# A linear-attention and SwiGLU kernel, whose hand-listed order of steps is replaced by another

## The chip, the cores and the metric

The kernel runs on one core of a Trainium2 chip. A core has five engines that work side by side: TensorE (PE, matrix multiply), VectorE (DVE), ScalarE (ACT), GpSimd (POOL) and SyncE (SP), and 16 DMA engines that move data. Each engine works through its own queue in order and waits at an instruction until what it needs is there. The metric is the device time of one execution in microseconds; less is better. Before the change the median of three runs is 202.34 us (202.3 to 202.5).

## The reference

Two stages. The first is a linear attention with a decaying state; the second is a gated feed-forward on its normalised output. There are 4 batches of 8 heads, 768 steps of time and heads of 48 columns, so 3,072 tokens of 384 columns; the feed-forward has 1,536 units.

```python
for t in range(S):                       # per batch and head
    cur = u * kt  (outer)  vt
    y[t] = rt @ (state + cur)
    state = wt[:, None] * state + kt (outer) vt
x  = y as [3072, 384]
xn = x / sqrt(mean(x*x) + 1e-6) * rms_g
out = (silu(xn @ w_gate) * (xn @ w_val)) @ w_out
```

## The kernel before

Time is cut into six superblocks (0 to 5) of 128 steps. A step of work is named `what.n.j`: n is the superblock, j the batch (0 to 3), or, in the feed-forward, one of 12 groups of 128 units. A superblock of 4 batches has 512 tokens, the width of one feed-forward matmul.

For each superblock and batch the attention goes through these steps. `load_r`, `load_k`, `load_v` and `load_w` (L241 to L266) fetch 128 x 384 numbers each, issued by SP; `load_w.0.j` fetches superblocks 0 and 1 at once (384 KB). `ln` (ACT) takes the logarithm of w, `cs_mm` (PE) sums it along time, `exp_r` and `exp_k` (ACT) raise the sums, `r_mul` (DVE) and `k_mul` (DVE, from superblock 1 on POOL) scale r and k by them. `w_tot` (DVE) keeps the decay of the whole block. r and k are turned: in superblocks 0 and 1 by `rk_pe` (PE transposes) and `rk_tr` (an ACT copy out of PSUM), later by a DMA transpose that SP issues, also called `rk_tr`. `q_mm` (PE) multiplies them, `q_mask_e`, `q_copy_o` and `q_mask_o` mask the product (DVE, ACT, and POOL or DVE), `cast_v` makes v bf16, `st_mm` and `st_new` carry the state to the next superblock, and `y_mm` (PE) forms the output. The term with u takes a way of its own: `bonus_mul` (two products on POOL, L452 and L453), `bonus_sum` (DVE), `bonus_v` (POOL); `x_add` (DVE) adds it. `x_sq`, `x_rstd` and `xn_mul` normalise; the result is turned by `xn_pe` and `xn_out` (PE, DVE), in superblocks 4 and 5 by `xn_tr` (DMA transpose on SP) and `xn_gain` (POOL, L586).

The feed-forward of superblock n needs all four turned batches. `gate_mm` and `val_mm` (L598) are three matmuls of 512 columns each, `silu` (ACT) and `h_mul` (DVE, L616) combine them, and `o_mm` (12 matmuls, L630), `o_out` and `out_dma` produce one batch of the output. The weights come in pieces that POOL issues: `load_gv.0.h` for groups 0 to 3 (384 KB as bf16; h is 0 for gate, 1 for val), `load_gv.1.h` for groups 4 to 11 (768 KB), and three `load_wo`. The source is float32 and the DMA casts it.

`warm` (L367) is a matmul of zeros into a PSUM bank that nobody reads.

The order is written out: the string `ORDER` lists all steps, a loop at the end of the kernel calls them one by one, and so every engine's queue has its steps in that order. Waits follow from the data and from the buffers: 8 each of r, k and v tiles, 4 of w, and eight PSUM banks in three rings, "a" and "b" with two banks, "q" with four. `psum` (L218) gives a step the bank of its ring whose last use lies furthest back in the order. ACT holds one function table at a time: logarithm and exponential share one, silu has another, and `act` loads it when needed (L229).

At the head of the old order, SP's queue is r.0.1, w.0.1, k.0.0, k.0.1, w.0.0, r.0.0, v.0.0, w.0.2, w.0.3, k.0.2, v.0.1, r.0.2, r.0.3, v.0.3, v.0.2, r.1.3, k.1.0, k.0.3 and then the rest of superblock 1. POOL's is bonus_mul.0.1, .0.0, .0.2, bonus_v.0.1, .0.0, bonus_mul.0.3, load_gv.0.1, bonus_v.0.2, load_gv.0.0, bonus_v.0.3, load_gv.1.0, k_mul.1.0, k_mul.1.1, load_gv.1.1. The first feed-forward steps of PE are val_mm.0.2, val_mm.0.3, one `warm`, gate_mm.0.2, gate_mm.0.3.

Of the kernel before, what the change touches and what calls it, by code (L numbers as in the profile page):

```python
# [25 lines left out]
load_r.0.1 load_w.0.1 load_k.0.0 load_k.0.1 ln.0.1 warm.31.0 load_w.0.0 ln.0.0 warm.0.0 warm.13.0 warm.28.0  # L26
bonus_mul.0.1 bonus_sum.0.1 load_r.0.0 load_v.0.0 bonus_mul.0.0 load_w.0.2 load_w.0.3 warm.29.0 load_k.0.2 load_v.0.1
load_r.0.2 bonus_mul.0.2 load_r.0.3 load_v.0.3 load_v.0.2 bonus_v.0.1 load_r.1.3 load_k.1.0 cs_mm.0.1 exp_k.0.1
warm.10.0 warm.17.0 warm.33.0 warm.38.0 exp_r.0.1 r_mul.0.1 k_mul.0.1 bonus_sum.0.0 bonus_v.0.0 cs_mm.0.0 exp_r.0.0
ln.0.2 exp_k.0.0 cast_v.0.0 r_mul.0.0 k_mul.0.0 w_tot.0.0 warm.8.0 warm.16.0 warm.12.0 warm.4.0 warm.30.0 w_tot.0.1  # L30
rk_pe.0.1 warm.15.0 warm.14.0 load_k.0.3 bonus_mul.0.3 load_r.1.1 load_r.1.0 load_k.1.1 load_v.1.1 load_r.1.2 ln.0.3
load_k.1.3 warm.20.0 warm.37.0 warm.2.0 warm.22.0 warm.23.0 warm.5.0 warm.3.0 rk_pe.0.0 warm.24.0 load_gv.0.1
load_k.1.2 load_v.1.0 load_w.2.1 warm.25.0 load_v.1.2 load_w.2.0 load_v.1.3 load_r.2.1 load_r.2.0 load_w.2.2 warm.32.0
warm.27.0 st_mm.0.0 st_new.0.0 load_w.2.3 cs_mm.0.2 rk_tr.0.1 q_mm.0.1 warm.19.0 rk_tr.0.0 exp_r.0.2 cast_v.0.1
r_mul.0.2 warm.7.0 cs_mm.0.3 q_mask_e.0.1 q_mm.0.0 warm.6.0 warm.18.0 warm.11.0 warm.26.0 warm.1.0 warm.21.0 warm.36.0
exp_k.0.2 w_tot.0.2 k_mul.0.2 rk_pe.0.2 q_mask_e.0.0 bonus_sum.0.2 bonus_v.0.2 exp_r.0.3 w_tot.0.3 q_mask_o.0.0
r_mul.0.3 warm.39.0 y_mm.0.0 warm.9.0 cs_mm.1.0 cast_v.0.3 q_mask_o.0.1 x_add.0.0 load_k.2.1 load_gv.0.0 cast_v.0.2
# [95 lines left out]
def kernel(  # L133
# [19 lines left out]
    DM = H * D  # L153
# [213 lines left out]
    def warm(n, j):  # L367
        ps = psum("q", ("warm", n, j), [128, DM])
        nc.tensor.matmul(ps.rearrange("p (a x) -> p a x", a=3), lhsT=zero, rhs=bc_mid(zero, 3), start=True, stop=True)
# [279 lines left out]
    for step in ORDER.split():  # L649
        fn, n, j = step.split(".")  # L650
# [32 lines left out]
```

## Time and profile before

| | |
|---|---|
| median of three runs | 202.34 us (202.3, 202.34, 202.5) |
| span of the profiled execution | 202.2 us, first to last instruction |
| PE busy | 192.6 us (95%), 1,600 matmuls |
| DVE, ACT, POOL busy | 146.1, 136.6, 134.3 us |
| read from and written to memory | 25.96 MB and 4.72 MB |
| loads and stores issued by SP | 28.58 MB, 119,504 packets |
| weights issued by POOL | 3.54 MB as written, 2,032 packets |

The profiled execution has no time of its own beside its span of 202.2 us; the runs lie 0.1 to 0.3 us above it.

A row of the timeline gives the start in microseconds from the first instruction, the duration, the engine, the line of the kernel, the operation, what is written and read, the shape, how many of the kind follow each other, and in brackets how long the engine had been idle and what ended that. SPq and POOLq are the queues that issue DMAs. Matmuls overlap in the pipeline, so the distance between the starts of two rows tells what a step costs TensorE, and not the duration of one. In the list of DMA issues the last number is the time from issue to landing. The chain of work that ended last is given as start, length and what it was.

### The profile page before, as it was taken

How to read it: one execution, taken by the hardware profiler on the slowest of the kernel's cores; microseconds unless marked ns; L12 is line 12 of the kernel's file. 1: busy time of each engine (PE TensorE's matmuls, PEld its weight loads, DVE VectorE, ACT ScalarE, POOL GpSimd, SP SyncE). 2: the span in 40 equal slices, each digit the busy share in tenths (PEclk: the TensorE clock that was granted, in tenths of full speed). 3: DMA queues.
4: the chain of work that ended last, by engine and by line, in shares of the span. 5: the costliest groups of instructions: out<-in, count | busy, mean ns of one | idle time of the engine just before them, and what ended most of it. 6: DMA issues, size and time to landing. Idle time of an engine off the chain costs nothing.

```text
span 202.2 us, 4444 instructions
## 1 busy us (share of the span) xinstructions
PE 192.6 (95%) x1600; PEld 113.5 (56%) x1600; DVE 146.1 (72%) x289; ACT 136.6 (68%) x278; POOL 134.3 (66%) x198
## 2 busy tenths in 40 slices
PE   1999988899999999999999999999999999999994
PEld 1564655455666555665556665555555555555562
DVE  6257796658999699987988889788878972146521
ACT  2577699688998557997566978679867764046300
POOL 6527599658789966899789898859898742400000
PEclk9999999999999999999999999999999999999999
DMA  6999999989999999958999978996184022103022
GB/s 152 243 244 177 209 182 202 202 161 201 199 192 221 196 179 238 225 133 194 177 231 245 206 171 195 216 241 134 24 192 112 15 68 71 45 3 117 0 97 99
DMA packets 121566, 32.41 MB, mean 160 GB/s; under 512 B 116420, under 2 KB 120392, under 8 KB 121544
## 3 DMA queue, kind: packets, MB, share of 16 engines
q1 hardware_dynamic: 119504, 28.58, 67.2%
q0 software_dynamic: 2032, 3.54, 9.7%
q8 instruction: 12, 0.20, 0.4%
q14 instruction: 10, 0.08, 0.1%
q10 hardware_dynamic: 8, 0.00, 0.0%
HBM read 25.96 MB, written 4.72 MB: 152 GB/s over the span
## 4 chain that ended last, share of the span: by engine, by line
PE 79%; SPq 8%; DMA 8%; POOL 2%; issue 1%; ACT 0%; POOLq 0%
PE ps_av L598 12%; PE ps_bu L598 12%; PE ps_bv L598 10%; PE ps_au L598 10%; PE ps_qx L630 8%; PE ps_qv L630 7%; SPq L244 7%; DMA wg_sb<-in_moe_w_gate_dram 6%; PE ps_qz L630 5%; PE ps_qu L630 3%; SPq L257 2%; DMA kt<-in_k_dram 2%; PE ps_qu L487 1%; PE ps_av L406 1%; PE ps_qu L515 1%
## 5 line engine op out<-in xcount | busy, mean ns | idle before, releaser
L630 PEld LDWEIGHTS <-ht 128*128 128x128 bf16 x300 | 28.3, 98 | 16.9
L231 ACT ACTIVATE sg<-ps_av 128x512 bf16<-128x512 f32 x38 | 22.7, 598 | 18.4 <-PE ps_av L598 16.8
L616 DVE TENSOR_TENSOR ht<-ps_bu,sg 128x512 bf16<-128x512 f32 x38 | 26.1, 686 | 11.7 <-PE ps_bu L598 8.4
L598 PEld LDWEIGHTS <-wg_sb 128*128 128x128 bf16 x216 | 22.8, 114 | 20.2 <-DMA wg_sb<-in_moe_w_gate_dram 2.1
L598 PEld LDWEIGHTS <-wv_sb 128*128 128x128 bf16 x216 | 23.2, 114 | 19.3 <-DVE xnt L580 0.2
L616 DVE TENSOR_TENSOR ht<-ps_bv,sg 128x512 bf16<-128x512 f32 x34 | 23.3, 686 | 12.2 <-PE ps_bv L598 8.8
L452 POOL TENSOR_TENSOR ruk<-rt,kt 128x384 f32<-128x384 f32 x24 | 24.0, 1000 | 11.1 <-DMA kt<-in_k_dram 6.0
L598 PE MATMUL ps_av<-xnt,wg_sb 128*128 128x512 bf16 x114 | 30.9, 380 | 0.4 <-DMA wg_sb<-in_moe_w_gate_dram 0.4
L231 ACT ACTIVATE sg<-ps_au 128x512 bf16<-128x512 f32 x34 | 20.4, 599 | 16.0 <-PE ps_au L598 14.6
L598 PE MATMUL ps_bu<-xnt,wv_sb 128*128 128x512 bf16 x114 | 30.9, 380 | 0.0
L598 PE MATMUL ps_au<-xnt,wg_sb 128*128 128x512 bf16 x102 | 27.7, 381 | 0.8 <-DMA wg_sb<-in_moe_w_gate_dram 0.8
L598 PE MATMUL ps_bv<-xnt,wv_sb 128*128 128x512 bf16 x102 | 27.7, 380 | 0.0
L453 POOL TENSOR_TENSOR ruk<-ruk,u_bc 128x384 f32<-128x384 f32 x24 | 23.9, 997 | 1.9
L462 POOL TENSOR_TENSOR ydiag<-vt,diag 128x384 f32<-128x384 f32 x24 | 19.7, 830 | 0.9 <-DVE diag L457 0.8
L446 POOL TENSOR_TENSOR rk<-kt,ek 128x384 bf16<-128x384 f32 x20 | 19.9, 1003 | 0.3 <-ACT ek L231 0.3
L505 POOL TENSOR_SCALAR_AFFINE_SELECT qts<-qts 128x512 bf16<-128x512 bf16 x20 | 12.5, 636 | 10.7 <-ACT qts L498 10.7
L630 PE MATMUL ps_qx<-wo_sb,ht 128*128 128x384 bf16 x96 | 16.9, 326 | 0.0
L630 PE MATMUL ps_qv<-wo_sb,ht 128*128 128x384 bf16 (+1 forms) x96 | 15.9, 316 | 0.0
L558 ACT ACTIVATE xn<-xb,rstd 128x384 bf16<-128x384 f32 x24 | 14.1, 608 | 1.2 <-POOL rstd L554 1.2
L457 DVE TENSOR_REDUCE diag<-ruk 128x8 f32<-128x384 f32 x24 | 12.9, 543 | 2.7 <-POOL ruk L453 2.7
L231 ACT ACTIVATE lw<-wt 128x384 bf16<-128x384 f32 (+1 forms) x20 | 11.2, 579 | 4.6 <-DMA wt<-in_w_dram 4.5
L229 ACT ACT_TABLE_LOAD x10 | 12.8, 1283 | 1.8 <-PEq L667 1.6
(153 smaller groups left out, 368.2 us busy)
## 6 DMA issues: line engine op xcount, KB each, us to landing
rt<-in_r_dram SPq DMA_DIRECT2D x24, 192.0 KB, 3.9
kt<-in_k_dram SPq DMA_DIRECT2D x24, 192.0 KB, 3.9
vt<-in_v_dram SPq DMA_DIRECT2D x24, 192.0 KB, 3.7
out_dram<-ob SPq DMA_DIRECT2D x23, 192.0 KB, 2.1
wt<-in_w_dram SPq DMA_DIRECT2D x16, 192.0 KB, 3.9
wt<-in_w_dram SPq DMA_DIRECT2D x4, 384.0 KB, 4.6
wo_sb<-in_moe_w_out_dram POOLq DMA_DIRECT2D x3, 384.0 KB, 5.2
wg_sb<-in_moe_w_gate_dram POOLq DMA_DIRECT2D x1, 768.0 KB, 12.0
```

The lines of the kernel that those rows point to most:

```text
L229: nc.scalar.preload_act_table_set(table_name)
L231: return nc.scalar.activation(**kw).ins
L244: dmas["load_" + which, n, j] = nc.sync.dma_start(out=inp[which, n, j], in_=t[j, :, n * L:(n + 1) * L, :].rearrange("h t d -> t h d")).ins
L446: eng.tensor_tensor(out=rk[:, n % 2, j, 1, :, 0:D], in0=inp["k", n, j], in1=bank["cs_k", n, j][:, 0:DM].rearrange("p (h d) -> p h d", h=H) ...
L452: nc.gpsimd.tensor_tensor(out=ruk[n, j], in0=inp["r", n, j], in1=inp["k", n, j], op=ALU.mult)
L453: nc.gpsimd.tensor_tensor(out=ruk[n, j], in0=ruk[n, j], in1=u_bc, op=ALU.mult)
L457: nc.vector.tensor_reduce(out=diag[n, j].rearrange("p h o -> p (h o)"), in_=ruk[n, j], axis=mybir.AxisListType.X, op=ALU.add)
L462: nc.gpsimd.tensor_tensor(out=ydiag[n, j], in0=inp["v", n, j], in1=diag[n, j].to_broadcast([128, H, D]), op=ALU.mult)
L558: nc.scalar.activation(out=xn, in_=xb[n, j], func=AF.Copy, scale=rstd[n, j][:, 1:2])
L598: nc.tensor.matmul(ps, lhsT=units(ws, c, f), rhs=xnt[n][:, c, :], start=(c == 0), stop=(c == KC - 1))
L616: nc.vector.tensor_tensor(out=ht[n][:, f, :], in0=bank.pop(("v", n, f)), in1=bank.pop(("sg", n, f)), op=ALU.mult)
L630: nc.tensor.matmul(ps[:, cols], lhsT=ht[n][:, f, b * L:(b + 1) * L], rhs=wo_sb[:, f, cols], start=(f == 0), stop=(f == FC - 1))
```

## The change

`ORDER` is replaced as a whole by one found under three sets of assumed transfer delays. Steps other than `warm` are the same set, each on the same engine; their order differs on every engine. There are 46 `warm` steps where there were 48. The second number of a `warm` step now names the ring whose bank it writes (0, 1, 2 for q, a, b), and the bank is taken as 512 columns wide, of which 384 are used as before.

The new queues begin so. SP: w.0.0, w.0.3, w.0.1, k.1.0, r.1.0, r.0.3, r.0.0, k.0.0, k.0.3, v.0.3, k.0.1, r.0.1, w.0.2, v.0.0, v.1.0, r.0.2, k.0.2, v.0.1, r.1.3, r.1.2, r.1.1, v.0.2, k.1.2, k.1.1, k.1.3, v.1.2, v.1.3, v.1.1. POOL: k_mul.1.0, bonus_mul.1.0, .0.0, .0.3, .0.1, bonus_v.0.3, .0.0, bonus_mul.0.2, q_mask_o.1.0, load_gv.0.0, bonus_v.0.1, k_mul.1.2, load_gv.0.1, bonus_v.1.0, .0.2, bonus_mul.1.2, load_gv.1.0, k_mul.1.1, k_mul.1.3, load_gv.1.1. PE begins with cs_mm.1.0, two `warm`, cs_mm.0.0, seven `warm`, rk_pe.1.0; its feed-forward begins with gate_mm.0.0, q_mm.1.2, rk_pe.1.1, val_mm.0.0, rk_pe.1.3, gate_mm.0.1, val_mm.0.1, val_mm.0.2, gate_mm.0.2, q_mm.1.1, q_mm.1.3, gate_mm.0.7, and four more gates before val_mm.0.8. ACT begins ln.0.0, ln.0.3, exp_r.0.0, exp_k.1.0, exp_r.1.0, exp_k.0.0, ln.0.1, rk_tr.1.0, exp_k.0.3, exp_r.0.3, exp_k.0.1. Around superblock 4's transposes SP has xn_tr.4.0, load_w.5.3, xn_tr.4.1, load_w.5.2, load_r.5.2, load_k.5.2, xn_tr.4.2, xn_tr.4.3, where it had xn_tr.4.0, load_v.5.1, load_v.5.0, xn_tr.4.1, .4.2, .4.3.

```diff
 ORDER = """
-load_r.0.1 load_w.0.1 load_k.0.0 load_k.0.1 ln.0.1 warm.31.0 load_w.0.0 ln.0.0 warm.0.0 warm.13.0 warm.28.0
-bonus_mul.0.1 bonus_sum.0.1 load_r.0.0 load_v.0.0 bonus_mul.0.0 load_w.0.2 load_w.0.3 warm.29.0 load_k.0.2 load_v.0.1
...
+load_w.0.0 ln.0.0 load_w.0.3 cs_mm.1.0 warm.0.0 warm.1.0 load_w.0.1 cs_mm.0.0 warm.2.0 warm.3.0 warm.4.0 warm.5.0
+warm.6.0 warm.7.0 warm.8.0 ln.0.3 exp_r.0.0 load_k.1.0 load_r.1.0 exp_k.1.0 k_mul.1.0 exp_r.1.0 load_r.0.3 r_mul.1.0
...
 """
...
     def warm(n, j):
-        ps = psum("q", ("warm", n, j), [128, DM])
+        ps = psum("qab"[j], ("warm", n, j), [128, 512])[:, 0:DM]
         nc.tensor.matmul(ps.rearrange("p (a x) -> p a x", a=3), lhsT=zero, rhs=bc_mid(zero, 3), start=True, stop=True)
```

203 lines of the change are left out of this document (102 added, 101 removed).

## The prediction

> **What bounds the kernel.** I read busy time by stretch first, then the chain that ended last, then the timeline of the first 45 us.
>
> ```profile
> core 0: us, PE busy (x) PEld busy (x) DVE busy (x) ACT busy (x) POOL busy (x), PEclk, DMA share, GB/s
> 33.20:40.00 6.80, 5.59 (x34) 2.53 (x32) 3.53 (x9) 5.32 (x8) 5.20 (x6) 1.00 1.14 203
> 40.00:120.00 80.00, 80.00 (x716) 48.35 (x717) 69.36 (x139) 62.32 (x128) 66.61 (x97) 1.00 1.02 198
> 120.00:199.30 79.30, 79.29 (x566) 45.81 (x563) 50.76 (x91) 46.08 (x93) 41.22 (x62) 1.00 0.41 103
> ```
>
> From 40.0 us to 199.3 us TensorE never waits, at full clock. So no reordering behind 40 us can gain; it can only lose. What can be won lies ahead of that.
>
> ```profile
> 27.90 11.95 DMA wg_sb<-in_moe_w_gate_dram
> 199.32 0.32 ACT ob L639
> ```
>
> ```profile
> 33.19 0.81 PE L598 MATMUL ps_bu<-xnt,wv_sb 128*128 128x512 bf16 x3
> 34.48 0.33 PE L369 MATMUL ps_qz<-zero 128*128 128x384 bf16 x1
> 35.64 0.84 PE L598 MATMUL ps_au<-xnt,wg_sb 128*128 128x512 bf16 x3 [0.83 <-DMA wg_sb<-in_moe_w_gate_dram]
> 38.06 0.81 PE L598 MATMUL ps_bu<-xnt,wv_sb 128*128 128x512 bf16 x3
> 38.71 0.81 PE L598 MATMUL ps_bv<-xnt,wv_sb 128*128 128x512 bf16 x3
> 39.90 0.84 PE L598 MATMUL ps_av<-xnt,wg_sb 128*128 128x512 bf16 x3 [0.38 <-DMA wg_sb<-in_moe_w_gate_dram]
> ```
>
> The chain ends with a copy at 199.32 and a store; the span is 202.2, so the tail is 2.9. The feed-forward begins at 33.19 (val_mm.0.2). One group of three matmuls takes 38.71 - 38.06 = 0.65 us for 1,536 columns, 0.42 ns a column; I price other TensorE steps by it. Between 33.19 and 40 TensorE waits twice, for weights: 35.64 - 34.48 - 0.16 = 1.0 (the 0.16 is the zero matmul) and 39.90 - 38.71 - 0.65 = 0.54. Real work from the first feed-forward step on is thus 199.32 - 33.19 - 1.0 - 0.54 - 0.16 = 164.4 us. The time is: start of the feed-forward + real work left + stalls + 2.9.
>
> **The change, part by part.** *Work left.* The steps are the same. Counting the PE queue, the changed order starts with gate_mm.0.0 and has by then done q_mm.1.0 and y_mm.1.0 more and st_mm.1.1 less: 512 + 768 - 384 = 896 columns, 0.4 us. Work left: 164.0.
>
> *Two zero matmuls less, others in other banks.* 2 x 0.16 = 0.3, in a stretch where TensorE waits anyhow: nothing. If that cover is gone, it is 0.3 at most.
>
> *Loads on SP.* Superblock 1's k, r and v of batch 0 come 4th, 5th and 15th; the last load of superblock 0, load_v.0.2, is 22nd, where before load_k.0.3 was 18th.
>
> ```profile
> 15.44 1.00 POOL L452 TENSOR_TENSOR ruk<-rt,kt 128x384 f32<-128x384 f32 x1 [4.09 <-DMA rt<-in_r_dram]
> 22.47 1.00 POOL L452 TENSOR_TENSOR ruk<-rt,kt 128x384 f32<-128x384 f32 x1 [3.39 <-DMA kt<-in_k_dram]
> 25.64 1.30 SPq L244 DMA_DIRECT2D vt<-in_v_dram  x1
> 30.66 6.49 SPq L244 DMA_DIRECT2D vt<-in_v_dram  x1
> ```
>
> POOL waited for the 12th load (r.0.2) until 15.44 and for the 18th (k.0.3) until 22.47: 1.17 us a load. By this k.0.2, 17th in the changed order, lands at about 21.3, v.0.2 at 26 to 27, k.1.2 (23rd) at about 27. v.0.2 is used by cast_v.0.2, which ScalarE (below) reaches at about 28, so its delay is covered by 1 to 2 us; past that each microsecond costs one.
>
> *Start of the feed-forward.* It needs the four normalised batches. I follow ScalarE, which carries exponentials, copies and norms of all of them.
>
> ```profile
> 5.94 0.50 PE L369 MATMUL ps_qx<-zero 128*128 128x384 bf16 x1
> 7.51 0.85 PE L391 MATMUL ps_au<-lw,mw 128*128 128x384 bf16 x2
> 9.01 0.53 PE L369 MATMUL ps_qz<-zero 128*128 128x384 bf16 x1
> 12.97 0.49 ACT L374 CAST vb<-vt 128x384 bf16<-128x384 f32 x1
> 13.37 0.84 ACT L231 ACTIVATE lw<-wt 128x768 bf16<-128x768 f32 x1
> 23.03 0.48 ACT L231 ACTIVATE ps_av<-ps_av 128x388 f32<-128x388 f32 x1
> 23.42 0.52 ACT L545 ACTIVATE junk<-xb 128x384 bf16<-128x384 f32 x1
> 24.06 0.29 ACT L231 ACTIVATE rstd<-rstd,eps_col 128x1 f32<-128x1 f32 x1
> 24.50 0.99 ACT L478 COPY rkT<-ps_qz 128x1024 bf16<-128x1024 bf16 x1
> 25.39 0.49 ACT L231 ACTIVATE ps_au<-ps_au 128x388 f32<-128x388 f32 x1
> 27.62 1.11 ACT L558 ACTIVATE xn<-xb,rstd 128x384 bf16<-128x384 f32 x2
> 29.20 0.55 DVE L580 TENSOR_TENSOR xnt<-ps_qv,gT 128x384 bf16<-128x384 bf16 x1
> 34.65 1.28 ACT L229 ACT_TABLE_LOAD   x1
> ```
>
> Starts of neighbouring rows give prices: cast 0.40, exponential 0.39, square sum 0.64, rstd 0.44, rkT copy 0.89; xn_mul 0.55, ln 0.84. TensorE is free at 5.94. cs_mm.1.0, two zeros at half pace (0.64) and cs_mm.0.0 (1.5 each, 9.01 - 7.51) bring exp_r.0.0 to 9.3, exp_k.1.0 ends at 10.15, k_mul.1.0 on POOL (1.0, the product of the 15.44 row) at 11.15; then rk_pe.1.0 (0.43), cs_mm.0.3 (0.65 by columns and 0.2 for its eight one-column matmuls, what 9.01 - 7.51 leaves over four of 0.32), six zeros (1.0), rk_pe.0.0 and cs_mm.0.1 make exp_k.0.1 ready at 15.0. From there to the last normalisation, xn_mul.0.2, ScalarE has 8 exponentials (3.1), 4 rkT copies (3.6), 5 casts (2.0), 1 ln (0.84), 1 mask copy (0.5), 4 square sums (2.6), 4 rstd (1.8), 4 xn_mul (2.2): 16.6 us, to 31.6, and about 1.0 of waiting (for cs_mm.0.2 and rk_pe.0.1): 32.6. Transposes (384 columns, 0.3 with their drain) and xn_out (0.55) with two handovers: gate_mm.0.0 at 33.6, 0.4 later than before. Bounds: 32.6 without those waits and with the zeros' 1.0 half won back, 35.5 when two loads come 2 us late.
>
> *Stalls after it: the weights.* POOL issues them, each behind steps that wait for loads.
>
> ```profile
> L505 POOL TENSOR_SCALAR_AFFINE_SELECT qts<-qts 128x512 bf16<-128x512 bf16 x20 | 12.5, 636 | 10.7 <-ACT qts L498 10.7
> 24.49 0.99 POOL L346 DMA_DIRECT2D wv_sb<-in_moe_w_val_dram  x1
> 26.29 0.81 POOL L346 DMA_DIRECT2D wg_sb<-in_moe_w_gate_dram  x1
> 30.63 0.80 POOL L346 DMA_DIRECT2D wv_sb<-in_moe_w_val_dram  x1
> wg_sb<-in_moe_w_gate_dram POOLq DMA_DIRECT2D x1, 768.0 KB, 12.0
> wv_sb<-in_moe_w_val_dram POOLq DMA_DIRECT2D x1, 768.0 KB, 13.5
> wv_sb<-in_moe_w_val_dram POOLq DMA_DIRECT2D x1, 384.0 KB, 7.5
> wg_sb<-in_moe_w_gate_dram POOLq DMA_DIRECT2D x1, 384.0 KB, 9.3
> ```
>
> The four landed at 32.0, 35.6, 39.9 and 44.1: 3.6 to 4.3 apart, one behind the other. On an empty queue I take 7.5 for a 384 KB piece and 7.5 + (4.3 - 3.6) = 8.2 for a 768 KB one; upper bound 12.0. In the changed order load_gv.0.0 stands behind bonus_mul.0.2 (22.47 to 24.49: 2.0) and a mask (636 ns): 21.3 + 2.0 + 0.6 = 23.9, landed 31.4, in time. load_gv.0.1 stands behind k_mul.1.2, so behind k.1.2: issued 27.5 (27.0 to 28.0), landed 35.0; val_mm.0.0 is reached at 33.6 + 0.65 + 0.65 (q_mm.1.2, rk_pe.1.1) + some 0.1: stall 0 to 0.5. load_gv.1.0 comes after two bonus_v (no more than a product's 1.0 each) and bonus_mul.1.2 (2.0), 4 us later: 31.5 where it was 27.90, landed 39.7 to 40.5; gate_mm.0.7 is reached at about 39.6: stall 0.1 to 0.9. load_gv.1.1 at 35, behind k_mul.1.1 and k_mul.1.3, lands at 44, when val_mm.0.8 is reached. ScalarE needs its table load (1.28) and rk_tr.1.3 in the same stretch; about 0.4, partly beside these. I take 1.0 in all; ends 0 and 3.5.
>
> *Behind 45 us.* Distances in the PE queue between a batch's y_mm, its transposes and the next feed-forward are like those of before; I price this at nothing, covered by slack of a microsecond or so.
>
> Sum: 33.6 + 164.0 + 1.0 + 2.9 = 201.5, against a span of 202.2. The runs (202.3 to 202.5, median 202.34) lie 0.1 above that span, so the forecast is **201.6**.
>
> **Rivals.** *Weights too late (slower).* load_gv.1.0 is issued 3.6 us later than before. If it takes the 12.0 of its row, it lands at 43.5 and gate_mm.0.7 stalls 3.9 where I counted at most 0.9 of 1.0: 201.6 + 3.0 = 204.6. It decides from 1.6 us of further delay on. For it: loads crawl while weights move (an issue took 6.49 at 30.66, 1.30 at 25.64), and load_gv.0.1 now waits for such a load while load_gv.0.0 moves. Against: half of the 12.0 was the wait for the piece ahead.
> The Trainium skill (DMA: Bandwidth & Descriptors, Queues, rings and completion order) has each DMA engine take turns between queue rows by packet, so small load packets share turns with large weight packets; the 6.49 row agrees. Its fit for one such transfer (the same page, Anatomy of one DMA), 2.0 us plus bytes over 436 GB/s, gives an estimate of 3.8 us for 768 KB; by that no weight stall is left and the sum would be 200.6, but the 7.5 of the half-size piece speaks against it.
>
> *Transposed batches of superblock 4 late (slower).*
>
> ```profile
> 146.76 0.58 SPq L244 DMA_DIRECT2D vt<-in_v_dram  x1
> 147.88 1.61 POOL L586 TENSOR_TENSOR xnt<-xnt,gT 128x384 bf16<-128x384 bf16 x2
> 149.54 0.81 PE L598 MATMUL ps_bv<-xnt,wv_sb 128*128 128x512 bf16 x3
> ```
>
> Before, the last gains end at 149.49 and the feed-forward uses them at 149.54: no room. The changed SP queue puts four loads (w.5.3, w.5.2, r.5.2, k.5.2) between the transposes, 4 x 0.58 = 2.3 on the queue, while the PE queue leaves only 0.3 more. If ScalarE has its rows no earlier, TensorE stalls 2.0: 203.6.
>
> *No difference.* The start comes at 34.3 instead of 33.6: 202.3. That is two more handovers on each of four batches; nothing excludes it.
>
> **How the numbers follow.** A difference under 0.2% (0.4 us) can't be told from none. Forecast (start 33.6 within 0.8, stalls under 1.3): 0.46, its own range 200.4 to 201.9; none: 0.20; weights late: 0.20; transposes late or another stall behind 45 us: 0.14. Faster 0.46, same 0.20, slower 0.34. Low end: start 33.0, no stalls, 200.0. High end 204.0 takes in the transposes and a weight stall of 2.4, and leaves out its full 3.0.
>
> **What would show it.** Right: first feed-forward matmul at 33 to 34.4, the last matmul 164 to 165.5 us later, TensorE filled from about 45 us on. Wrong: ScalarE waiting for a load between 15 and 32 us; a gate or val group waiting over 1.3 us for weights; TensorE idle at the first group of superblock 4 or 5.

## The result and the profile after

The changed kernel takes 204.22 us (median of four runs, 203.80 to 204.86), the kernel before beside it 202.42 us (202.3 to 202.94): a ratio of 1.0083 with a 95% interval of [1.0055, 1.0111]. Forecast were 201.6 us and a small gain; it is 0.8% slower, and outside the range of 200.0 to 204.0. In later runs of both (e13 below) the two stood at 204.78 and 203.46 us, a ratio of 1.0106 [1.0047, 1.0165]. (The ratios leave out executions over 1.5% above the fastest of their kernel and the medians don't, so a ratio can differ from the quotient of two medians; the profiles of e10 and e17 are of such executions.)

From the page of the changed kernel: span and count, busy time of the engines, and the shares of the chain that ended last.

```profile
span 202.5 us, 4452 instructions
PE 192.0 (95%) x1598; PEld 113.9 (56%) x1598; DVE 146.5 (72%) x289; ACT 141.7 (70%) x282; POOL 134.8 (67%) x198
PE 82%; ACT 6%; DVE 4%; DMA 3%; POOL 2%; issue 1%; POOLq 0%; DVEq 0%
```

This execution took 204.26 us as a run. So its time lies 1.76 above its span, and so it is for the other three (203.8 and 202.1, 204.18 and 202.5, 204.86 and 203.1). The prediction took 0.1. That is the first part of the miss.

Busy time by stretch (after the start and end of the stretch its length, then the engines, TensorE's granted clock, the share of DMA and GB/s), the same stages as in the prediction, the first from the start of the feed-forward on:

```profile
35.10:40.00 4.90, 4.73 (x40) 2.71 (x41) 2.58 (x6) 4.87 (x9) 4.80 (x6) 1.00 1.13 208
40.00:120.00 80.00, 79.84 (x690) 47.93 (x690) 70.13 (x138) 66.49 (x130) 58.73 (x89) 1.00 0.91 188
120.00:199.40 79.40, 79.36 (x567) 45.86 (x564) 50.17 (x90) 45.46 (x92) 45.80 (x66) 1.00 0.45 109
```

Behind 40 us TensorE is again full at full clock. The timeline of TensorE shows where the time went:

```profile
11.48 0.37 PE L370 MATMUL ps_qx<-zero 128*128 128x384 bf16 x1
17.30 0.32 PE L370 MATMUL ps_qu<-zero 128*128 128x384 bf16 x1 [1.11 <-ACT rkT L479]
19.96 0.50 PE L392 MATMUL ps_au<-lw,mw 128*128 128x384 bf16 x2
35.07 0.81 PE L599 MATMUL ps_au<-xnt,wg_sb 128*128 128x512 bf16 x3
39.97 0.81 PE L599 MATMUL ps_au<-xnt,wg_sb 128*128 128x512 bf16 x3 [0.17 <-ACT sg L232]
56.66 0.81 PE L631 MATMUL ps_qx<-wo_sb,ht 128*128 128x384 bf16 x4 [0.16 <-DMA wo_sb<-in_moe_w_out_dram]
```

The chain ends with this piece of TensorE (start, length):

```profile
198.44 1.00 PE ps_qv L631 x12
```

The first feed-forward matmul (gate_mm.0.0) starts at 35.07, where 33.6 was forecast and the kernel before starts at 33.19. From there to the end of the last matmul it is 199.44 - 35.07 = 164.4 us, all small stalls included; forecast were 164.0 of work and 1.0 of stalls. So the second part of the miss is the start, forecast 1.5 too early, and what comes behind it (0.63 less work and stalls, 0.16 more tail) gives 0.5 back. 1.66 + 1.47 - 0.5 is the 2.6 us between 201.6 and 204.2.

ScalarE in the head, with its two waits between exp_k.0.1 (15.45) and the last normalisation, xn_mul.0.2 (33.32):

```profile
15.45 0.47 ACT L232 ACTIVATE ps_bv<-ps_bv 128x384 f32<-128x384 f32 x1 [1.35 <-PE ps_bv L399]
20.73 0.48 ACT L232 ACTIVATE ps_au<-ps_au 128x388 f32<-128x388 f32 x1 [1.02 <-issue]
23.28 1.01 ACT L479 COPY rkT<-ps_qu 128x1024 bf16<-128x1024 bf16 x1 [0.47 <-PE ps_qu L470]
33.32 0.61 ACT L559 ACTIVATE xn<-xb,rstd 128x384 bf16<-128x384 f32 x1
```

The step at 20.73 is exp_r.0.2; it waits for cs_mm.0.2, which TensorE reaches only at 19.96, behind twelve zero matmuls of which the third waited 1.11 us for a PSUM bank (17.30). The step at 23.28 is rk_tr.0.1.

POOL with k_mul.1.2 (26.74) and the four weight pieces, and below the time from issue to landing of each piece:

```profile
24.09 0.98 POOL L347 DMA_DIRECT2D wg_sb<-in_moe_w_gate_dram  x1
26.74 1.00 POOL L447 TENSOR_TENSOR rk<-kt,ek 128x384 bf16<-128x384 f32 x1 [0.80 <-ACT ek L232]
27.68 0.81 POOL L347 DMA_DIRECT2D wv_sb<-in_moe_w_val_dram  x1
32.12 0.80 POOL L347 DMA_DIRECT2D wg_sb<-in_moe_w_gate_dram  x1
35.74 0.80 POOL L347 DMA_DIRECT2D wv_sb<-in_moe_w_val_dram  x1
```

```profile
wg_sb<-in_moe_w_gate_dram POOLq DMA_DIRECT2D x1, 768.0 KB, 7.5
wv_sb<-in_moe_w_val_dram POOLq DMA_DIRECT2D x1, 768.0 KB, 9.6
wg_sb<-in_moe_w_gate_dram POOLq DMA_DIRECT2D x1, 384.0 KB, 5.5
wv_sb<-in_moe_w_val_dram POOLq DMA_DIRECT2D x1, 384.0 KB, 6.5
```

No matmul of the feed-forward waits for gate or val weights in this execution.

### The profile page after: what moved, and what is told of

The parts are those of the page before. It is cut to its first block, busy times and chain, and to the rows that moved or that the text cites. A ratio compares the mean times of both kernels' runs of the same rounds, so it can differ in the third digit from the quotient of the medians.

```text
span 202.5 us, 4452 instructions
## 1 busy us (share of the span) xinstructions
PE 192.0 (95%) x1598; PEld 113.9 (56%) x1598; DVE 146.5 (72%) x289; ACT 141.7 (70%) x282; POOL 134.8 (67%) x198
## 4 chain that ended last, share of the span: by engine, by line
PE 82%; ACT 6%; DVE 4%; DMA 3%; POOL 2%; issue 1%; POOLq 0%; DVEq 0%
PE ps_av L599 11%; PE ps_au L599 11%; PE ps_bv L599 10%; PE ps_bu L599 9%; PE ps_qu L631 7%; PE ps_qx L631 6%; PE ps_qv L631 5%; PE ps_qz L631 4%; DMA wo_sb<-in_moe_w_out_dram 3%; ACT rkT L479 1%; ACT sg L232 1%; DVE qts L495 1%; PE ps_qu L370 1%; DVE qts L503 1%; PE ps_qu L536 1%
## 5 line engine op out<-in xcount | busy, mean ns | idle before, releaser
L617 DVE TENSOR_TENSOR ht<-ps_bv,sg 128x512 bf16<-128x512 f32 x38 | 26.1, 687 | 9.5 <-PE ps_bv L599 4.9
L599 PE MATMUL ps_bv<-xnt,wv_sb 128*128 128x512 bf16 x114 | 30.9, 380 | 0.0
L617 DVE TENSOR_TENSOR ht<-ps_bu,sg 128x512 bf16<-128x512 f32 x34 | 23.4, 687 | 10.2 <-PE ps_bu L599 7.6
L232 ACT ACTIVATE sg<-ps_au 128x512 bf16<-128x512 f32 x37 | 22.2, 599 | 12.0 <-PE ps_au L599 10.1
L599 PE MATMUL ps_au<-xnt,wg_sb 128*128 128x512 bf16 x111 | 30.0, 379 | 0.2 <-ACT sg L232 0.2
L599 PE MATMUL ps_av<-xnt,wg_sb 128*128 128x512 bf16 x105 | 28.5, 380 | 0.0
L599 PE MATMUL ps_bu<-xnt,wv_sb 128*128 128x512 bf16 x102 | 27.7, 380 | 0.0
L546 ACT ACTIVATE junk<-xb 128x384 bf16<-128x384 f32 x24 | 12.5, 521 | 4.6 <-DVE xb L541 4.5
L631 PE MATMUL ps_qx<-wo_sb,ht 128*128 128x384 bf16 x84 | 15.0, 326 | 0.2 <-DMA wo_sb<-in_moe_w_out_dram 0.2
L631 PE MATMUL ps_qu<-wo_sb,ht 128*128 128x384 bf16 x84 | 14.8, 326 | 0.0
```

What stands on the lines that cost most here:

```text
L232: return nc.scalar.activation(**kw).ins
L599: nc.tensor.matmul(ps, lhsT=units(ws, c, f), rhs=xnt[n][:, c, :], start=(c == 0), stop=(c == KC - 1))
L617: nc.vector.tensor_tensor(out=ht[n][:, f, :], in0=bank.pop(("v", n, f)), in1=bank.pop(("sg", n, f)), op=ALU.mult)
L631: nc.tensor.matmul(ps[:, cols], lhsT=ht[n][:, f, b * L:(b + 1) * L], rhs=wo_sb[:, f, cols], start=(f == 0), stop=(f == FC - 1))
```

## The experiments

Theory at the outset: zero matmuls stand in TensorE's queue ahead of steps that ScalarE waits for. Rivals: the head is bound by ScalarE's own work and order, by loads, or the zeros are needed for the clock; and beside all this the base of the sum was wrong. All runs in one view; the start is that of the first feed-forward matmul in the profiled execution, the times are medians with lowest and highest, and "before" is the unchanged kernel before on the same chip. A profile shows one execution, which can lie anywhere in the range: that of e11 took 205.18 us, that of e12 took 202.29, the least of its twelve. The diffs below name the steps that move with a few neighbours; steps in between are left out.

| run | edit | start | time, us | before | ratio to before |
|---|---|---|---|---|---|
| e0 | kernel before | 33.13 | 203.23 (202.69 to 204.45) | 203.03 | 1.0005 [0.9978, 1.0031] |
| e1 | no zeros 15-26 | 36.06 | 205.66 (204.75 to 208.41) | 203.03 | 1.0109 [1.0058, 1.0159] |
| e2 | no zeros 15-45 | 38.23 | 208.41 (207.02 to 208.82) | 203.03 | 1.0238 [1.0193, 1.0282] |
| e4 | e2, cs_mm.0.2 early | 38.56 | 207.45 (207.02 to 210.82) | 203.03 | 1.0195 [1.0149, 1.0241] |
| e5 | no zeros 22-26 | 34.57 | 205.14 (204.84 to 207.81) | 203.79 | 1.0108 [1.0054, 1.0161] |
| e8 | no zeros 9-14, 22-26 | 35.86 | 205.69 (203.89 to 208.66) | 203.79 | 1.0067 [1.0027, 1.0107] |
| e6 | rk_tr.0.1 early | 34.99 | 204.51 (204.06 to 207.91) | 203.79 | 1.0067 [1.0027, 1.0106] |
| e10 | e8 + e6 + load_wo.2.0 early | 37.11 | 205.97 (203.59 to 208.19) | 203.79 | 1.0043 [1.0005, 1.0081] |
| e13 | changed kernel | 35.37 | 204.78 (204.51 to 207.93) | 203.46 | 1.0106 [1.0047, 1.0165] |
| e14 | k_mul.1.2 later | 35.19 | 203.98 (203.57 to 205.80) | 203.46 | 1.0037 [1.0005, 1.0070] |
| e11 | e8 + k_mul.1.2 later | 33.36 | 203.96 (203.00 to 205.40) | 203.46 | 1.0041 [1.0009, 1.0073] |
| e12 | e10 + k_mul.1.2 later | 33.16 | 203.52 (202.29 to 205.03) | 203.46 | 1.0030 [1.0000, 1.0060] |
| e16 | no zeros 9-14, k_mul.1.2 later | 33.47 | 204.70 (203.41 to 205.75) | 203.19 | 1.0069 [1.0042, 1.0096] |
| e15 | e12 + load_gv.1.0 earlier | 33.19 | 206.61 (205.68 to 208.51) | 203.19 | 1.0189 [1.0141, 1.0236] |
| e17 | e15 + load_v.1.0 later | 37.38 | 207.57 (202.84 to 208.78) | 203.19 | none given |
| e18 | e17 + order on ScalarE | 38.65 | 207.50 (206.46 to 209.07) | 203.19 | 1.0223 [1.0178, 1.0268] |
| e20 | e16 + two loads first | 33.45 | 203.96 (203.50 to 205.05) | 203.08 | 1.0050 [1.0024, 1.0076] |
| e19 | e12 + two loads first | 33.16 | 203.89 (202.77 to 204.46) | 203.08 | 1.0028 [1.0005, 1.0051] |

**The base of the sum.** The kernel before, profiled once more.

> The kernel before, unchanged, profiled once more. Theory A (the profiled execution of before was a slow one of its kind: its span of 202.2 belongs to a time near 203.9, because in the changed kernel every time lies 1.7 us above its span): this profile has a span of 200.4 to 201.0 with a time of 202.1 to 202.7, 1.7 apart, the 1.5 us are missing from the stretch ahead of 40 us (start of the feed-forward or its first stalls), and the last matmul group again comes with no wait behind 40 us. Rival B (the distance of time and span differs from kernel to kernel, 0.1 before and 1.7 after): span 202.0 to 202.4 with a time of 202.1 to 202.6, and the stages lie where they lay in the first profile.

The profiled execution has a span of 201.6 at a time of 203.31, 1.71 apart; the twelve executions all have 1.66 to 1.75 between span and time (204.45 and 202.7, 202.69 and 201.0). TensorE at the start of the feed-forward:

```profile
33.13 0.81 PE L598 MATMUL ps_bu<-xnt,wv_sb 128*128 128x512 bf16 x3
34.67 0.84 PE L598 MATMUL ps_au<-xnt,wg_sb 128*128 128x512 bf16 x3
38.94 0.84 PE L598 MATMUL ps_av<-xnt,wg_sb 128*128 128x512 bf16 x3 [0.22 <-DMA wg_sb<-in_moe_w_gate_dram]
```

It starts as in the first profile (33.13 and 33.19), but the gate group that waited for its weights until 35.64 there starts at 34.67 here. Theory A holds for the distance: by it a span of 202.2 belongs to a time of 203.9, so the prediction added its steps to an execution 1.5 us slower than the median. Of these 1.5, this profile shows 0.97 at that gate group, as weights that come late in one execution and not in another, and 0.6 at the end of the span; one at 202.3 was never profiled, so the rest isn't shown. Beside this second profile the changed kernel starts 1.94 later (35.07 against 33.13) and takes 1.09 less from there to the copy that ends last (164.45 against 165.54): that is the 0.9 us between their spans.

**Zeros out of TensorE's queue, and the clock.** First the twelve ahead of q_mm.0.3:

```diff
-warm.15.0 warm.16.0 warm.17.0 warm.18.0 warm.19.0 warm.20.0
-warm.21.0 warm.22.0 warm.23.0 warm.24.0 warm.25.0 warm.26.0
 bonus_mul.0.1 rk_tr.0.3 bonus_sum.0.3 bonus_v.0.3 w_tot.0.1 q_mm.0.3
```

> The changed kernel without the twelve zero matmuls warm.15 to warm.26; their product is read by nobody. Theory 1 (the zeros stand in TensorE's queue ahead of real steps and one of them waits 1.1 us for the PSUM bank that ScalarE still copies from): q_mm.0.3 starts at 18.2 instead of 19.02, cs_mm.0.2 at 19.4 instead of 19.96, exp_r.0.2 at 20.1 instead of 20.73, the feed-forward at 34.4 instead of 35.07, time 203.6, which is 0.6 below the changed kernel. Rival 2 (without them the granted TensorE clock falls in the stretch behind 16 us): the real steps there run at half pace, cs_mm.0.2 takes over 1.4 us instead of 0.9, the feed-forward starts at 35.5 or later, time 204.6 or more.

Rival 2 came out. TensorE's timeline, and its busy time and granted clock (fourth number) by stretch:

```profile
17.66 0.28 PE L487 MATMUL ps_qx<-rkT 48*128 48x128 bf16 x1 [2.34 <-ACT rkT L478]
18.62 0.50 PE L369 MATMUL ps_au<-zero 128*128 128x384 bf16 x1
```

```profile
18.00:20.00 2.00, 2.00 (x21) 0.50 0.67 129
22.00:24.00 2.00, 2.00 (x27) 0.50 1.06 210
24.00:26.00 2.00, 1.26 (x19) 0.98 1.09 206
```

q_mm.0.3 does start earlier (17.66), but after 2.34 us without work TensorE runs at half clock until 24 us, and its steps there cost double. Leaving out all zeros from 15 on, and moving cs_mm.0.2 up as well, fails in the same way:

```diff
-warm.15.0
...
-warm.45.2
```

> The changed kernel without the 31 zero matmuls warm.15 to warm.45. Theory 1: the waits of warm.16 (1.1), warm.29 (0.73), warm.35 and what they hold up go; the feed-forward starts at 33.9 instead of 35.07 and the time is 203.0. Rival 2 (the clock falls): granted clock below 0.9 between 16 and 36 us, steps of TensorE at half pace there, start of the feed-forward at 36 or later, time 205 or more. If neither moves the start by more than 0.3, the waits of the zeros were hidden and the head is bound by ScalarE's own work.

```diff
 exp_k.0.1 exp_r.0.1
+ln.0.2
...
 rk_pe.0.3
+cs_mm.0.2
```

> As the one without warm.15 to warm.45, and with ln.0.2 moved up in ScalarE's queue to behind exp_r.0.1 and cs_mm.0.2 in TensorE's to behind rk_pe.0.3, so that exp_r.0.2 finds its sums ready. Theory 1: ScalarE's 1.02 of idle time ahead of exp_r.0.2 goes, exp_r.0.2 starts at 19.7, the feed-forward at 33.3, time 202.4. Rival 2: as there, 205 or more. Rival 3 (loads: w of batch 2 has not landed by 16.7 us): ScalarE waits for wt and the gain stays below 0.3 beside the kernel without the zeros.

The granted clock is 0.51 and 0.50 from 18 to 20 us, and the start moves to 38.23 and 38.56 (in e4 ln.0.2 also waits 0.79 for its w, so rival 3 had a part). So not all zeros after 15 us can go. Next five, and then eleven:

```diff
-warm.22.0 warm.23.0 warm.24.0 warm.25.0 warm.26.0
```

> The changed kernel without the last five of the twelve zero matmuls ahead of q_mm.0.3 (warm.22 to warm.26; nobody reads their product). With seven left TensorE is never idle for more than the 1.3 us for which warm.16 waits, against 2.4 us in the kernel without all twelve, after which the clock had fallen to half. Theory 1 (zeros in the queue delay the real steps as long as the clock stays up): clock 1.0 from 16 to 24 us, q_mm.0.3 at 18.25 instead of 19.02, cs_mm.0.2 at 19.35 (then it waits for ln.0.2), the feed-forward 0.6 earlier at 34.5, time 203.6. Rival 2 (the clock falls here too): half pace behind 18 us, time 205 or more. Rival 4 (from 19 us on ScalarE and VectorE are full anyway): the matmuls start earlier but the feed-forward stays at 35.0, time 204.2.

```diff
-warm.9.0 warm.10.0 warm.11.0 warm.12.0 warm.13.0 warm.14.0
 rk_tr.1.0 exp_k.0.3
...
-warm.22.0 warm.23.0 warm.24.0 warm.25.0 warm.26.0
```

> As the one without warm.22 to warm.26, and also without the six zeros warm.9 to warm.14 that stand 1.0 us long ahead of rk_pe.0.0 and cs_mm.0.1. Theory 1: exp_k.0.1 starts at 14.45 instead of 15.45, all of ScalarE's queue behind it moves up, the feed-forward starts at 33.7, time 202.9. Rival 2: the clock falls in the gaps, time 205 or more. Rival 4: the start moves by less than 0.5, time 204.0.

ScalarE in e5, then POOL in e5, then VectorE and POOL in e8:

```profile
14.90 0.47 ACT L232 ACTIVATE ps_bv<-ps_bv 128x384 f32<-128x384 f32 x1 [1.34 <-PE ps_bv L399]
19.55 0.48 ACT L232 ACTIVATE ps_au<-ps_au 128x388 f32<-128x388 f32 x1 [0.40 <-ACT vb L375]
31.61 0.52 ACT L546 ACTIVATE junk<-xb 128x384 bf16<-128x384 f32 x1 [0.92 <-DVE xb L541]
```

```profile
27.58 1.00 POOL L447 TENSOR_TENSOR rk<-kt,ek 128x384 bf16<-128x384 f32 x1 [1.84 <-ACT xn L559]
```

```profile
31.91 0.56 DVE L540 TENSOR_TENSOR xb<-ps_qv,ydiag 128x384 f32<-128x384 f32 x1 [2.23 <-POOL ydiag L462]
```

```profile
28.48 1.00 POOL L446 TENSOR_TENSOR rk<-kt,ek 128x384 bf16<-128x384 f32 x1 [3.24 <-DMA kt<-in_k_dram]
```

In e5 the clock stays up, and exp_r.0.2 starts at 19.55 instead of 20.73: 0.55 of that because this execution's clock came up earlier (exp_k.0.1 at 14.90 instead of 15.45), 0.63 by the five zeros, as theory 1 has it. But x_sq.0.2 then waits 0.92 for x_add.0.2 (31.61). k_mul.1.2 waits 1.84 on POOL; the releaser named, a normalisation, is no input of it, and in e6, where it starts at 27.57, the same wait is for its load. And behind 40 us e5 loses 0.65 to val weights (45.82) and 1.14 to superblock 4's transposed batches (150.68), and its time is 205.14. In e8 the wait is 2.23 on VectorE, for ydiag, which is bonus_v.0.2 of POOL. That stands behind k_mul.1.2, and k_mul.1.2 waits for the load of k.1.2 until 28.48. A second chain lies right behind the first: load, POOL, VectorE. It was not among the expectations.

**ScalarE's order.** All zeros kept, rk_tr.0.1 moved to where ScalarE idles; and then everything together.

```diff
-q_mm.0.3 q_mm.0.0 warm.27.1 warm.28.1
+q_mm.0.3 rk_pe.0.1 warm.27.1 warm.28.1
...
-ln.0.2 cs_mm.0.2 q_mm.1.0 q_mask_o.0.0 cast_v.0.0
+ln.0.2 cast_v.0.0 rk_tr.0.1 cs_mm.0.2 q_mm.0.0 q_mask_o.0.0 q_mm.1.0
...
-y_mm.0.3 rk_pe.0.1 load_r.1.1
+y_mm.0.3 load_r.1.1
...
-exp_r.1.2 rk_tr.0.1 x_add.0.3
+exp_r.1.2 x_add.0.3
```

> The changed kernel with all its zeros; only rk_pe.0.1 is moved up on TensorE to directly behind q_mm.0.3, its copy rk_tr.0.1 on ScalarE to behind cast_v.0.0, where ScalarE stood idle for 1.02 us, and q_mm.0.0 back to behind cs_mm.0.2. Theory 5 (a good part of the lost time is the order on ScalarE: it stands idle while work is ready): the idle 1.02 ahead of exp_r.0.2 and 0.47 ahead of rk_tr.0.1 are filled, the feed-forward starts 0.6 to 1.2 earlier, at 33.9 to 34.5, time 203.0 to 203.6. Rival 6 (VectorE, without a pause from 19.5 us on, bounds the batches from there): the start moves by less than 0.3, time 204.2.

```profile
15.14 0.47 ACT L232 ACTIVATE ps_bv<-ps_bv 128x384 f32<-128x384 f32 x1 [1.35 <-PE ps_bv L399]
23.73 0.52 ACT L546 ACTIVATE junk<-xb 128x384 bf16<-128x384 f32 x1 [1.10 <-DVE xb L541]
24.71 0.52 ACT L546 ACTIVATE junk<-xb 128x384 bf16<-128x384 f32 x1 [0.37 <-DVE xb L541]
```

The waits of 1.02 and 0.47 go (0.30 is left) and waits of 1.10 and 0.37 for VectorE's x_add come: the start stays at 34.99, as rival 6 has it. Theory 5 falls.

```diff
-warm.9.0
...
-warm.14.0
...
-warm.22.0
...
-warm.26.0
...
 load_wo.1.0
+load_wo.2.0
```

> The two edits together (rk_tr.0.1 earlier; warm.9 to warm.14 and warm.22 to warm.26 out), and load_wo.2.0 issued directly behind load_wo.1.0, so that o_mm.0.0 doesn't wait 0.32 us for it. Theories 1 and 5 together: feed-forward at 33.0, time 202.0, 0.4 below the kernel before. If only one of them holds: 202.9 to 203.3. If the clock falls: 205 or more.

Here k_mul.1.2 starts at 29.74 after a wait of 4.52 for its load, VectorE waits 3.42 for ydiag, and the start slips to 37.11.

**k_mul.1.2 out of the way on POOL.** The changed kernel beside it for comparison.

> The changed kernel, unchanged, profiled once more beside the next three. Theory 7 (the head ends at k_mul.1.2: it waits on POOL for load_k.1.2, the 23rd load, and holds up bonus_v.0.2, x_add.0.2, xn_mul.0.2 and gate_mm.0.0 behind it): 204.2, where k_mul.1.2 starts at 26.7 the feed-forward starts at 35.07, and for each microsecond that it starts later than 27 the feed-forward starts one later. Rival: the start doesn't follow k_mul.1.2.

```diff
-k_mul.1.2
 load_gv.0.1 bonus_v.1.0 bonus_v.0.2
+k_mul.1.2
```

> The changed kernel with one step moved: k_mul.1.2 behind load_gv.0.1, bonus_v.1.0 and bonus_v.0.2 in POOL's queue. Theory 7: alone it brings little where the load is in time (204.0 to 204.2; the feed-forward at 34.9 to 35.07), since ScalarE is full from 23.3 us on; the spread between executions gets smaller. If POOL's order were the whole loss: feed-forward at 34.3 or earlier, 203.4. Rival (contention): load_gv.0.1, issued 2 us earlier, slows the loads of k.1.2 and after, rk_pe.1.2 waits, 204.6.

> The kernel without warm.9 to warm.14 and warm.22 to warm.26, and with k_mul.1.2 moved behind bonus_v.0.2. Theory 7 with theory 1: VectorE's 2.23 us of waiting for ydiag (x_add.0.2) go, and so does the half clock after it; the feed-forward starts at 33.7, wv for val_mm.0.8 is then 0.5 late, time 203.1 to 203.3. If theory 7 is wrong: the feed-forward at 35.5 or later, time 205.

> The kernel with all three edits (rk_tr.0.1 earlier, the eleven zeros out, load_wo.2.0 earlier), and with k_mul.1.2 moved behind bonus_v.0.2. Theory 7 with 1 and 5: VectorE's wait of 3.42 us goes; the feed-forward at 33.3 to 33.7, time 202.4 to 203.0. If theory 7 is wrong: as without the move, feed-forward behind 36, 205.5.

In e13 the zero matmuls still run at half pace at 11.46 and exp_k.0.1 starts at 15.75; k_mul.1.2 at 27.06, the feed-forward at 35.37, all three 0.3 later than in the first profile; so this run can't tell theory 7 from the clock. e14 is 0.8 us below e13 in the median, more than expected, and all but one of its runs lie between 203.57 and 204.42; where the 0.8 comes from the two profiles don't show (starts of 35.37 and 35.19, times of 204.51 and 204.34). With the eleven zeros out as well (e11) the start comes to 33.36, 2.0 earlier than e13, and with the rest to 33.16. Of the 2.0 the six zeros of warm.9 to warm.14 are 0.98, and most of the rest is the clock, which is up by 9.29 us in e11. So these steps, and the clock, are what made the head late. But e11 then waits 1.92 for the gate weights (41.65), and its median of 203.96 is that of e14 (203.98). In the median e12 regains 1.26 of the 1.3 us to the kernel before, and doesn't pass it.

**Which zeros, and why the gain is not kept.** Only the six:

> The changed kernel without the six zero matmuls warm.9 to warm.14 alone, and with k_mul.1.2 behind bonus_v.0.2 (so that the late load of k.1.2 doesn't hide the effect); the twelve of warm.15 to warm.26 stay. Theory 1a (the six zeros ahead of rk_pe.0.0 and cs_mm.0.1 are the larger part): exp_k.0.1 at 14.0 instead of 15.5, feed-forward at 34.0, time 203.0 to 203.4. Theory 1b (the five of warm.22 to 26 are the larger part): feed-forward at 34.8 or later, 203.8. Without the six and the five it was 33.36.

ScalarE, TensorE, and POOL of e16:

```profile
13.85 0.47 ACT L231 ACTIVATE ps_bv<-ps_bv 128x384 f32<-128x384 f32 x1 [0.37 <-PE ps_bv L398]
```

```profile
9.55 0.33 PE L369 MATMUL ps_qu<-zero 128*128 128x384 bf16 x1
33.47 0.81 PE L598 MATMUL ps_au<-xnt,wg_sb 128*128 128x512 bf16 x2
41.30 0.84 PE L598 MATMUL ps_av<-xnt,wg_sb 128*128 128x512 bf16 x2 [1.57 <-DMA wg_sb<-in_moe_w_gate_dram]
150.13 0.81 PE L598 MATMUL ps_bv<-xnt,wv_sb 128*128 128x512 bf16 x2 [0.71 <-POOL xnt L586]
```

```profile
30.16 1.00 POOL L446 TENSOR_TENSOR rk<-kt,ek 128x384 bf16<-128x384 f32 x1 [2.28 <-DMA kt<-in_k_dram]
33.13 0.80 POOL L346 DMA_DIRECT2D wg_sb<-in_moe_w_gate_dram  x1
```

exp_k.0.1 (13.85) and the start (33.47) are both 1.6 earlier than in the first profile of the changed kernel. 0.98 of that is the six zeros (6 x 0.163), which stood between cs_mm.0.3 and rk_pe.0.0; 0.6 is the clock, which was up by 9.55 here and only behind 11.48 there. Theory 1a holds, and yet the time is 204.70, as high as the changed kernel. 2.3 us are lost again in two places: the gate weights (issued at 33.13, since POOL waits for k.1.2 until 30.16) are 1.57 late at gate_mm.0.7, and superblock 4's last transposed batch is 0.71 late. In the first profile of the changed kernel neither waits; in e13 the second does:

```profile
149.80 0.81 PE L599 MATMUL ps_bv<-xnt,wv_sb 128*128 128x512 bf16 x3 [0.31 <-POOL xnt L587]
```

Five more try to keep the gain. The weights first:

```diff
 bonus_v.0.2
+load_gv.1.0
 k_mul.1.2 bonus_mul.1.2
-load_gv.1.0
```

> As the kernel with all three edits and k_mul.1.2 moved, and load_gv.1.0 issued directly behind bonus_v.0.2, ahead of k_mul.1.2 and bonus_mul.1.2, so that the gate weights no longer stand behind the load of k.1.2. Theory 8 (what spreads that kernel from 202.3 to 205.0 is the wait for wg: 1.92 us in the kernel that had its k.1.2 at 30.2): the wait at gate_mm.0.7 goes, median 202.6 to 203.0, highest below 204. Rival (the weights then slow the loads, contention): k.1.2 lands later, rk_pe.1.2 and gate_mm.0.0 behind it wait, 204 or more.

POOL and TensorE of e15:

```profile
27.57 0.80 POOL L346 DMA_DIRECT2D wg_sb<-in_moe_w_gate_dram  x1
37.59 0.99 POOL L446 TENSOR_TENSOR rk<-kt,ek 128x384 bf16<-128x384 f32 x1 [5.19 <-ACT junk L545]
```

```profile
38.64 0.40 PE L469 MATMUL ps_qz<-ident,rk 128*128 128x128 bf16 x4 [2.89 <-POOL rk L446]
```

The rival, contention: with a third piece of weights under way from 27.57 on, k_mul.1.3 can start only at 37.59, where it started at 34.80 in the changed kernel and at 34.02 in e12. Its exponential is ready at 32.8, so what it waits for is the load of k.1.3, as in e12, where that wait is 1.66 (the releaser named, a square sum, has nothing to do with it). TensorE waits 2.89 for rk_pe.1.3 behind it.

```diff
-load_v.1.0
 load_r.0.2 load_k.0.2 load_v.0.1 load_r.1.3 load_r.1.2 load_r.1.1 load_v.0.2 load_k.1.2
+load_v.1.0
```

> As the one before, and load_v.1.0 moved on SP from 15th to behind load_k.1.2, a part of loading batch 0 of superblock 1 first undone: eight loads that superblock 0 and k.1.2 need move up by one, 1.0 to 1.2 us. Theory 7 (k.1.2's load is the late one): k.1.2 lands 1 us earlier, k_mul.1.2 never waits over 0.3, time 202.4 to 202.8 and a smaller spread. Rival: nothing waits for these loads any more, as the one before within 0.2.

```diff
-exp_r.1.2 x_sq.0.3 x_sq.0.0 cast_v.0.1 x_rstd.0.3 exp_k.1.2
+exp_r.1.2 cast_v.0.1 x_sq.0.3 exp_k.1.2 x_sq.0.0 x_rstd.0.3
```

> As the one before, and on ScalarE cast_v.0.1 moved ahead of x_sq.0.3 and exp_k.1.2 ahead of x_sq.0.0, into the 0.77 and 0.37 us that ScalarE waits for VectorE's x_add. Theory 1 (ScalarE's queue sets the start of the feed-forward once the zeros are out of the way): feed-forward 0.6 to 0.8 earlier, at 32.4, time 201.8 to 202.2, below the kernel before. Rival: VectorE's x_add or the weights (load_gv.0.1 for val_mm.0.0) take over, no change to the one before.

Neither keeps it. POOL and ScalarE in e18:

```profile
30.77 1.61 POOL L462 TENSOR_TENSOR ydiag<-vt,diag 128x384 f32<-128x384 f32 x2 [4.80 <-DMA vt<-in_v_dram]
30.71 0.51 ACT L374 CAST vb<-vt 128x384 bf16<-128x384 f32 x1 [4.43 <-DMA vt<-in_v_dram]
```

The first of these two products is bonus_v.1.0, the cast is cast_v.1.0; they stand ahead of bonus_v.0.2 and cast_v.0.2 in their queues and need v.1.0, the load that e17 moved back. SP issues it at 23.68 in e18 (22.84 in e17), and it is in place only at 30.7 (28.7). So the move made a load late that was in use sooner than supposed. The times of e17, 202.84 to 208.78, suggest that the same kernel can have it in time or not. After the wait TensorE runs at half clock (0.50 from 34 to 36 us), and e18 can't tell whether ScalarE's order mattered. Last, the two loads that were late, three places up:

```diff
+load_v.0.2 load_k.1.2
 load_r.1.3 load_r.1.2 load_r.1.1
-load_v.0.2 load_k.1.2
```

> As the kernel without warm.9 to warm.14 and with k_mul.1.2 moved (feed-forward at 33.47, 1.57 us of waiting for wg at gate_mm.0.7, 204.7), and on SP load_v.0.2 and load_k.1.2 moved ahead of load_r.1.3, load_r.1.2 and load_r.1.1, 3 places up. Theory 9 (with the zeros gone it is the loads of v.0.2 and k.1.2, issued just ahead of the first weights, that end the head and hold the later weights up on POOL): k_mul.1.2 doesn't wait for its load, load_gv.1.0 is issued by 31.5 instead of 33, the wait at gate_mm.0.7 falls below 0.5, time 203.2 to 203.6. Rival (the r loads now are the late ones, bonus_mul.1.2 waits for r.1.2 just as long): 204.5 or more.

> The repaired kernel (rk_tr.0.1 earlier, eleven zeros out, load_wo.2.0 earlier, k_mul.1.2 moved; 203.5, spread 202.3 to 205.0) with the same move of load_v.0.2 and load_k.1.2. Theory 9: its spread shrinks and the median comes to 202.4 to 202.8, 0.4 to 0.8 below the kernel before on the same chip. Rival (r loads late instead): 203.5 or more.

e20's TensorE at superblock 4, and POOL's last two gains there (`xn_gain`, which wait for the transposes) in e20 and in e12:

```profile
148.93 0.81 PE L598 MATMUL ps_bv<-xnt,wv_sb 128*128 128x512 bf16 x3 [0.95 <-POOL xnt L586]
```

```profile
147.26 1.61 POOL L586 TENSOR_TENSOR xnt<-xnt,gT 128x384 bf16<-128x384 bf16 x2 [1.67 <-DMA xnt<-xn]
```

```profile
145.95 1.61 POOL L586 TENSOR_TENSOR xnt<-xnt,gT 128x384 bf16<-128x384 bf16 x2 [0.68 <-DMA xnt<-xn]
```

Theory 9 is half right: k.1.2 and the weights of gate_mm.0.7 come in time, e20 falls by 0.7 to 203.96 (in the ratio from 1.0069 to 1.0050), and runs lie closer together. What is won is lost at 148.93, where POOL waits 1.67 for the transposes; in e12 (202.29 us) POOL waits 0.68 and TensorE not at all. This wait is not one of an early head: of the eighteen profiles of the changed order thirteen have it, from 0.18 to 1.39, e8 with its start at 35.86 the longest, and neither of the two of the kernel before. Whether the four loads that now stand between these transposes on SP cause it, no run tested. e19 stays at 203.89. No kernel beat the one before.

## Why the prediction was wrong

**The bound.** Right: TensorE has no gap that counts behind 40 us in the first profiles, before and after, and the time is start + work + stalls + tail.

**Work left, two zeros less.** 164.0 was right within what the small waits leave open (164.4 with all stalls). The loss of two zeros in itself is nothing.

**"The runs lie 0.1 above that span".** This step failed, and it is the largest term: 1.66 us. Every execution that has both on record, of every kernel here, takes 1.66 to 1.79 longer than its span. So the profile was of an execution near 203.9, 1.5 above the median. Of the 1.5 of weight stalls that the sum took out of it, 0.97 are not there in the second profile of the same kernel: nothing that the change could win. With 1.7 in place of 0.1 the same sum gives 203.2, slower than 202.34 and not faster, so this step turned the direction too.

**The start, 33.6.** Failed by 1.47. exp_r.0.0 (9.14, forecast 9.3) was right. exp_k.0.1 came at 15.45 instead of 15.0: the prediction let rk_pe.1.0 follow k_mul.1.0 at 11.15 and put the seven zeros ahead of it at nothing, but the clock rose only between 11.48 and 11.68, and at half pace they held rk_pe.1.0 until 11.68. ScalarE's work was 17.0 instead of 16.6 (33.93 - 15.45 less two waits), its waits 1.49 instead of 1.0, and the last step 1.14 instead of 1.0. The bounds, 32.6 to 35.5, held it; the value was taken too near the lower one. The wait for cs_mm.0.2 was foreseen, not its size: the zeros queue for a bank that ScalarE still reads.

**Loads.** In time in the changed kernel, as said. By the prediction's own 1.17 us a load k.1.2 lands at 28.3, though, and not at 27; it was used at 26.74 in the first profile and waited for until 28.48 in e8. The cover was judged on the wrong user: not cast_v.0.2 on ScalarE but bonus_v.0.2 on POOL, behind k_mul.1.2 and its load, is the tight one (e5, e8, e10).

**Weight stalls, 1.0.** They were not there. The issues were right to 0.75 (24.09, 27.68, 32.12, 35.74 against 23.9, 27.5, 31.5, 35), the pieces were 0.7 to 2.0 faster than priced for three of four, and the late start gave them time as well. The fit in the Trainium skill (DMA: Bandwidth & Descriptors, Anatomy of one DMA), 3.8 us for 768 KB as an estimate, gave the right outcome with a wrong duration: 7.5 and 9.6 were measured.

**Rivals.** "No difference" (start 34.3) came nearest. "Weights too late" didn't happen in the changed kernel, but it did where its head was mended and POOL waited for k.1.2 (1.57 in e16, 1.92 in e11; not in e12). "Transposes late" is real as well, up to 1.39 and not 2.0: nothing in the first profile of the changed kernel, 0.31 in e13. What one wait gives another can absorb; the prediction priced them one at a time.

## What to carry to other kernels

Before summing steps on a profiled execution, set its time beside its span, and that time beside the median: a stall that only the profiled execution has can't be won. Where several chains end within a microsecond of each other, here zeros on TensorE, loads on POOL, weights and transposes, a step taken off one is worth only the distance to the next; look for the waits that vanished because something else was late. Zero matmuls that hold the clock up belong where nobody waits behind them, and how many can go is limited by the clock, which can fall where TensorE then stands idle. Before a load is moved back, look for its first user on every queue.

## What the runs showed of the hardware

The clock of TensorE rises at a moment that differs between executions of nearly the same head: the zeros run at full pace from 9.55 us in e16, while in e13 they still take 0.52 at 11.46 (TensorE's first matmul starts at about 4.2 in all). Through rk_pe.1.0 this moves the head: with the same steps of TensorE ahead of it, exp_k.0.1 starts at 14.84 in e4 and at 15.75 in e13. The clock fell to half after 2.34 us without work in e1, and in e8 and e17 where the longest gaps shortly before were 1.53 and 1.11, while in e15 a gap of 2.89 left it up, so the length of one gap doesn't decide it:

```profile
38.00:40.00 2.00, 1.36 (x10) 1.00 0.71 140
```

The Trainium skill (TensorE: Matmul & The Clock Gate, Part 1: The HAM clock gate) explains such a dependence by a window of 3.4 us that runs on regardless of the kernel; the runs agree that the moment varies, but by 2.2 us and not by the 0.5 either way that it gives, and the fall came after less than a window without work.

A weight piece that POOL issued earlier made a load of SP later by as much or more: with the piece issued at 27.57 instead of 30.52 (e15 against e12, one profile each), k_mul.1.3 was held back from 34.02 to 37.59. The Trainium skill (DMA: Bandwidth & Descriptors, Queues, rings and completion order) has each DMA engine take turns between queues by packet; the direction agrees, the packets themselves no run here shows.
